# Taking one half-size dummy matmul out of the opening of an MLP kernel, between the transposes and layer 1

## The chip, the cores and the metric

The kernel runs on one core of one Trainium2 chip. The metric is device time in microseconds (us) for one execution; where several runs are compared, the mean or the median over runs is given and named. Early in execution the pace of the matmuls doubles (in the trace, pairs of 256 columns start 213 ns apart at first and 109 ns apart later) while the granted clock reads 1.0 throughout. "The clock doubles" means this change of pace below; whether it is a clock, no trace shows.

## The reference

```python
def reference(x, w1, b1, w2, b2):          # x: 1 x 2048 x 448, w1: 448 x 1792, w2: 1792 x 448, all bf16
    h = jnp.einsum("bsd,df->bsf", x, w1) + b1
    h = jax.nn.gelu(h, approximate=True)
    return jnp.einsum("bsf,fd->bsd", h, w2) + b2
```

## The kernel before

The 2048 tokens are worked in four chunks of 512. For the first chunk, x comes in its natural layout and is transposed on TensorE (twelve 128x128 transposes, and two more for the 64 remainder columns of D = 3 x 128 + 64). ScalarE and VectorE copy ("evacuate") the results from PSUM, where the kernel has TensorE put them, to SBUF, from where its layer matmuls read them. All layer matmuls then run as pairs on the two 64-row halves of the array (in the trace the two of a layer-1 pair start 2 to 6 ns apart).

While x is on its way, TensorE runs dummy matmuls of ones (from 0.78 us in the trace; x landed at 3.86). One more half-size dummy (256 columns) stands after the transposes.

```python
    HC = SC // 2          # 256; SC = 512
    NWARM = 7
    # ...
        def turn_b1():    # bias into its layout, on VectorE
            for q in range(4):
                pr.op("vector", lambda e, q=q: e.transpose(
                    b1t[32 * q:32 * q + 32, :], b1n[:, 32 * q:32 * q + 32]), after=["b1n"], event=("b1t", q))
            pr.op("vector", lambda e: e.tensor_copy(b1_f[:, :], b1t[:, 0:NFT]),
                  after=[("b1t", q) for q in range(4)], event="b1")

        def warm(n, cols=SC):
            for _ in range(n):
                pr.op("tensor", lambda e: e.matmul(unit[0][:, 0, 0:cols], lhsT=ones_w, rhs=ones_m[:, 0:cols],
                                                   start=True, stop=True))
    # ... in turn_all(): four x tiles, their evacuation on VectorE, ScalarE, VectorE, ScalarE in turn
            for t in range(STC):
                turn(t)
                evac(("vector", "scalar")[t % 2], t)
    # ... the two remainder transposes (L359), and their copies (L368)

        warm(NWARM)
        warm(1, HC)
        turn_all()
        warm(1, HC)       # the dummy in question
        turn_b1()

        for i in (0, 1):  # remainder weights, copied to the other 64 rows, on VectorE (L382)
            # ...
            pr.op("vector", lambda e, odd=odd: e.tensor_copy(odd(slice(0, H)), odd(slice(H, P))),
                  after=[("w1r", i)], event=("w1rU", i))
        L = [Layer1(0, j) for j in range(NPAIR)]
        for h in (0, HC):         # first the columns of x tiles 0 and 1, then those of 2 and 3
            L[0].a(h, h + HC)
            L[1].a(h, h + HC)
        L[0].b()                  # its first steps are on w1; the last of them needs the copied remainder weights
        # ...
```

Of the kernel before, what the change touches and what calls it, by code (L numbers as in the profile page):

```python
# [73 lines left out]
def bass_standalone__dense_activation_gelu__prompt_kernel(  # L74
# [13 lines left out]
    HC = SC // 2  # L88
# [9 lines left out]
    with ExitStack() as es:  # L98
# [79 lines left out]
        def turn_b1():  # L178
# [5 lines that stand above are left out]
# [5 lines left out]
# [4 lines that stand above are left out]
# [156 lines left out]
        def turn_all():  # L349


            pr.op("vector", lambda e: e.tensor_copy(  # L352
                xr[:, :, :].rearrange("p q (two h) -> p q two h", two=2),
                xn[:, :, D3:D].rearrange("p (q two) h -> p q two h", two=2)), after=["x"], event="xr_in")
# [3 lines that stand above are left out]
            for q in range(STC // 2):  # L358
                pr.op("tensor", lambda e, q=q: e.transpose(  # L359
                    stage(0)[:, q * P:(q + 1) * P], xr[:, q, :], ident[:, :]),  # L360
                    after=["xr_in", ("xT0", 0)], event=("xr", q))
            halves = (slice(0, H), slice(H, P))
            for src, engine in enumerate(("vector", "scalar")):
                i = stage(0)[halves[src], 0:2 * P].rearrange("p (q s) -> p q s", q=2)
                for dst in (src, 1 - src):
                    o = xT[halves[dst], KT, 0:SC].rearrange("p (q two s) -> p q two s", q=2, two=2)[:, :, src, :]
                    pr.op(engine, lambda e, o=o, i=i, engine=engine:
                          e.copy(o, i) if engine == "scalar" else e.tensor_copy(o, i),  # L368
                          after=[("xr", 0), ("xr", 1)], event=("xR0", dst, src))
            busy[(3, 0)] = ("xR0", 1, 0)  # L370
            busy[(3, 2)] = ("xR0", 0, 1)
# [1 line left out]
        warm(NWARM)  # L373
        warm(1, HC)
        turn_all()
        warm(1, HC)
        turn_b1()

        for i in (0, 1):
# [78 lines left out]
```

## Time and profile before

| | value |
|---|---|
| time, median of the 3 first runs | 94.28 us (94.17 to 94.35) |
| profiled execution | 94.75 us, span 93.4 us |
| TensorE (PE) busy | 90.4 us, 97% of the span |
| last transpose starts | 5.337 us |
| dummy starts | 5.444 us |
| first layer-1 matmul starts | 5.794 us |
| first matmul on the remainder weights starts (its twin, on the copied rows, 2 ns later) | 8.155 us |

The starts with three digits are single records of the trace; the views below show the same to 0.01 us.

The page of the kernel before begins with the busy time of each engine (us, share of the span, number of instructions):

```profile
span 93.4 us, 2060 instructions
## 1 busy us (share of the span) xinstructions
PE 90.4 (97%) x932; PEld 46.5 (50%) x932; DVE 13.3 (14%) x33; ACT 38.5 (41%) x63; POOL 1.7 (2%) x8
```

The chain of work that ended last, in order of time, for the kernel before (start, length, what):

```profile
7 pieces in order of time: start us, us, what
0.74 0.04 issue
0.78 3.36 PE u L191 x8
4.14 1.29 PE u L338 x12
5.43 0.21 PE u L359 x2
5.65 0.21 PE u L191
5.86 85.41 PE u L216 x909
91.27 0.38 DVE out_sb L325
```

Dummies (L191), transposes (L338, L359), the dummy in question (L191 again, 0.21 us), then layer matmuls (L216): but for the short first and last pieces it is all TensorE. So the dummy stands on this chain.

The timeline of the kernel before around the dummy (start, length, engine, line, operation; in brackets the idle time before it and what ended that):

```profile
5.23 0.42 PE L359 MATMUL u<-ident,xr 128*128 128x128 bf16 x2
5.34 0.15 PEld L191 LDWEIGHTS u<-const-bfloat16-1.0 128*128 128x128 bf16 x1
5.44 0.42 PE L191 MATMUL u<-const-bfloat16-1.0 128*128 128x256 bf16 x1
...
5.79 0.13 PEld L216 LDWEIGHTS u<-xT,w_sb 64*128 64x128 bf16 x4 [0.30 <-issue]
5.79 0.40 PE L216 MATMUL u<-xT,w_sb 64*128 64x256 bf16 x2
```

A matmul's length in this view overlaps the next one's (0.42 us for a dummy that takes 0.21 us of the chain), so distances between starts are what count. The weight load of layer 1 is late, after 0.30 us of idle on the loader, and the profile names nothing that it waited for.

### The profile page before, as it was taken

The numbers are of one execution on the slowest core, as the hardware profiler recorded it, in microseconds if no ns is written. First come the engines' busy times: TensorE is split into PE (matmuls) and PEld (weight loads), VectorE is DVE, ScalarE is ACT, GpSimd is POOL, SyncE is SP. The second block draws the span as 40 slices with busy tenths as digits, with TensorE's granted clock in tenths as the row PEclk, the third lists the DMA queues.
The fourth block names the chain that finished last, engine by engine and source line by source line (L and its number), as shares of the span: only waits on it lengthen the run. The fifth ranks groups of instructions, "written<-read, shape, count | busy, mean of one in ns | idle before, by whom it ended". The sixth has DMA issues, their size and how long they took to land.

```text
span 93.4 us, 2060 instructions
## 1 busy us (share of the span) xinstructions
PE 90.4 (97%) x932; PEld 46.5 (50%) x932; DVE 13.3 (14%) x33; ACT 38.5 (41%) x63; POOL 1.7 (2%) x8
## 2 busy tenths in 40 slices
PE   6999999999999999999999999999999999999990
PEld 2475444455544444454554444445544444475890
DVE  0173001010334000000234000000234000000421
ACT  6073787900002887900002888900001878910001
POOL 6000000000000000000000000000000000000000
DMA  2999999554748000000033000000022000000022
GB/s 51 358 275 292 360 309 151 113 113 91 83 86 217 7 0 0 7 0 0 0 102 101 0 0 4 0 7 0 0 98 98 0 0 7 0 0 7 18 80 98
DMA packets 12344, 7.32 MB, mean 78 GB/s; under 512 B 6960, under 2 KB 12144, under 8 KB 12336
## 3 DMA queue, kind: packets, MB, share of 16 engines
q1 hardware_dynamic: 11904, 6.80, 31.1%
q10 hardware_dynamic: 400, 0.39, 1.2%
q8 instruction: 7, 0.11, 0.5%
q14 instruction: 1, 0.01, 0.0%
q0 software_dynamic: 32, 0.00, 0.0%
HBM read 3.79 MB, written 1.84 MB: 60 GB/s over the span
## 4 chain that ended last, share of the span: by engine, by line
PE 97%; DVE 0%; issue 0%
PE u L216 91%; PE u L191 4%; PE u L338 1%; DVE out_sb L325 0%; PE u L359 0%
## 5 line engine op out<-in xcount | busy, mean ns | idle before, releaser
L268 ACT ACTIVATE g<-u,b_f 128x512 bf16<-128x512 f32 x56 | 35.0, 685 | 40.3 <-PE u L216 40.3
L216 PE MATMUL u<-w_sb,g 64*128 64x448 bf16 (+1 forms) x504 | 43.2, 328 | 0.0
L216 PE MATMUL u<-xT,w_sb 64*128 64x512 bf16 (+1 forms) x348 | 41.2, 372 | 0.0
L216 PEld LDWEIGHTS u<-w_sb,g 64*128 64x128 bf16 x504 | 24.4, 94 | 18.6
L216 PEld LDWEIGHTS u<-xT,w_sb 64*128 64x128 bf16 x348 | 16.9, 95 | 19.6 <-issue 0.3
L311 DVE TENSOR_TENSOR out_sb<-u,b_bc 128x448 bf16<-128x448 f32 x14 | 8.1, 619 | 60.6 <-PE u L216 60.6
L216 PE MATMUL u<-xT,w1r 64*128 64x512 bf16 x56 | 10.6, 376 | 0.0
L191 PE MATMUL u<-const-bfloat16-1.0 128*128 128x512 bf16 (+1 forms) x9 | 3.8, 578 | 0.8 <-PEq L443 0.8
L216 PEld LDWEIGHTS u<-xT,w1r 64*128 64x128 bf16 x56 | 2.7, 94 | 3.3
L328 ACT CAST out_sb<-u 128x224 bf16<-128x224 f32 x1 | 0.3, 346 | 9.2 <-PE u L216 9.2
L191 PEld LDWEIGHTS u<-const-bfloat16-1.0 128*128 128x128 bf16 x9 | 1.2, 138 | 2.4 <-issue 2.4
L345 ACT COPY xT<-u 128x384 bf16<-128x384 bf16 x2 | 1.0, 479 | 2.8 <-PE u L338 2.8
L175 ACT ACT_TABLE_LOAD x1 | 1.3, 1283 | 0.7 <-PEq L443 0.7
L338 PEld LDWEIGHTS u<-ident,xn 128*128 128x128 bf16 x12 | 1.2, 140 | 0.5 <-issue 0.5
L338 PE MATMUL u<-ident,xn 128*128 128x128 bf16 x12 | 1.4, 307 | 0.0
L186 DVE COPY xT<-xT 64x512 bf16<-64x512 bf16 x3 | 0.9, 290 | 3.5 <-DMA xT<-in_x_dram 3.5
L406 DVE COPY b_z<-b_bc 1x448 bf16<-1x448 bf16 x1 | 0.3, 267 | 6.8 <-DMA b_bc<-in_b_dram 6.8
L319 DVE TENSOR_TENSOR out_sb<-u,b_bc 128x448 bf16<-128x448 f32 x1 | 0.6, 625 | 1.7 <-PE u L216 1.7
L180 DVE STREAM_TRANSPOSE b1t<-b1n 32x32 bf16<-32x32 bf16 x4 | 0.8, 202 | 0.1
L345 DVE COPY xT<-u 128x384 bf16<-128x384 bf16 x2 | 0.7, 357 | 0.7 <-PE u L338 0.7
L368 ACT COPY xT<-u 64x256 bf16<-64x256 bf16 x2 | 0.7, 368 | 0.0
L352 DVE COPY xr<-xn 128x256 bf16<-128x256 bf16 x1 | 0.2, 227 | 3.0 <-DMA xn<-in_x_dram 3.0
(18 smaller groups left out, 5.0 us busy)
## 6 DMA issues: line engine op xcount, KB each, us to landing
out_dram<-out_sb SPq DMA_DIRECT2D x16, 112.0 KB, 1.7
w_sb<-in_w_dram SPq DMA_DIRECT2D x2, 784.0 KB, 8.7
w_sb<-in_w_dram SPq DMA_DIRECT2D x1, 576.0 KB, 6.4
xn<-in_x_dram SPq DMA_DIRECT2D x1, 448.0 KB, 3.1
w_sb<-in_w_dram ACTq DMA_DIRECT2D x1, 384.0 KB, 4.2
w_sb<-in_w_dram SPq DMA_DIRECT2D x1, 384.0 KB, 4.1
xT<-in_x_dram SPq DMA_TRANSPOSE x12, 4.5
w1r<-in_w_dram SPq DMA_DIRECT2D x1, 160.0 KB, 4.0
```

What stands on the lines that cost most here:

```text
L175: pr.op("scalar", lambda e: e.activation(junk[:, :], one, ACT.Gelu_apprx_tanh), event="table")
L180: pr.op("vector", lambda e, q=q: e.transpose(b1t[32 * q:32 * q + 32, :], b1n[:, 32 * q:32 * q + 32]), after=["b1n"], event=("b1t", q))
L186: pr.op("vector", lambda e: e.tensor_copy(xT[0:H, KT, s0:s1], xT[H:P, KT, s0:s1]), after=after, event=event)
L191: pr.op("tensor", lambda e: e.matmul(unit[0][:, 0, 0:cols], lhsT=ones_w, rhs=ones_m[:, 0:cols], start=True, stop=True))
L216: o = pr.op("tensor", lambda e: e.matmul(unit[u][:, lo, cols], lhsT=lhsT, rhs=rhs, start=start, stop=stop, skip_group_check=skip), after=a ...
L268: pr.op("scalar", lambda e, lo=lo, ft=ft: e.activation(g[:, ft, c * SC:(c + 1) * SC], unit[u][:, lo, :], ACT.Gelu_apprx_tanh, bias=b1_f[:, ...
L311: pr.op("vector", lambda e, lo=lo, j=j: e.tensor_tensor(out=out_sb[:, j, :], in0=unit[u][:, lo, 0:D], in1=b2_bc[:, :], op=ALU.add), after= ...
L319: pr.op("vector", lambda e: e.tensor_tensor(out=out_sb[:, j, :].rearrange("p (two h) -> p two h", two=2), in0=unit[u][:, :, 0:DH], in1=b2_ ...
L328: pr.op("scalar", lambda e: e.copy(out_sb[:, j, DH:D], unit[u][:, 1, 0:DH]), after=[y[1]], event=("o", j, 1))
L338: pr.op("tensor", lambda e, k=k: e.transpose(stage(t)[:, k * P:(k + 1) * P], xn[:, t, k * P:(k + 1) * P], ident[:, :]), after=["ident", "x ...
L345: pr.op(engine, lambda e: e.copy(o, i) if engine == "scalar" else e.tensor_copy(o, i), after=[("xt", t)], event=("xT0", t))
L368: e.copy(o, i) if engine == "scalar" else e.tensor_copy(o, i),
```

## The change

One line goes. The intent is to have layer 1 start earlier by what the dummy took.

```diff
         warm(NWARM)
         warm(1, HC)
         turn_all()
-        warm(1, HC)
         turn_b1()
```

The order of the instructions on the other engines stays as it was. Line numbers below it fall by one (L382 becomes L381).

## The prediction

> **What bounds the kernel now.** TensorE. Its busy line reads 90.4 of 93.4 us (97%); the chain that ended last is 97% TensorE. In the groups, the layer matmuls show 0.0 us of idle before them, their weight loads 0.3 us before the first. A nanosecond taken from the opening of TensorE reaches the end, unless something else holds the work.
>
> **What is removed.** One dummy matmul (ones, 128x256) and its weight load, between the last transpose and the first layer-1 matmul. Nothing is added; the other engines keep their instructions in the same order.
>
> **Its place, from the timeline between 5.2 and 8.6 us.** The last transpose starts at 5.34 us, the dummy at 5.44, the first layer-1 matmul at 5.79, 350 ns later. 256-column pairs at the same slow pace start 208 to 213 ns apart, so the dummy streams some 213 ns, and about 137 ns more pass. What the first layer-1 matmul needs is there earlier: the first w1 part landed at 4.99 us, ScalarE's evacuation ended at 5.31, the wait for it at 5.40. [...]this weight load starts only at 5.79, when elsewhere one starts with the matmul before. The drain would then follow the last transpose, and layer 1 start near 5.58 us, 0.21 earlier.
>
> **The clock.** The granted clock reads 1.00 throughout, but the pairs are 208 ns apart up to 6.62 us and 107 ns from 6.74 on. [...] If the doubling stays near 6.7 us, the 0.21 us gained is slow time: it holds one 256-column pair, worth 107 ns at the full rate. That is my central case: 0.11 us. If the doubling moves forward with the work, 0.21 us is offered.
>
> **The next limit.** VectorE copies the remainder weights of layer 1 to the other 64 rows after the bias; the copy ends at 7.85 us; the weight load that needs it starts at 7.94, its matmul at 8.155. VectorE does not move. 0.11 us earlier just fits (8.05); 0.21 us would lose about 0.1 to this wait. Both cases come to about 0.1 us.
>
> **Prediction.** 94.28 - 0.11 = 94.17, rounded up for a little waiting: **94.18 us**, range 93.95 to 94.50. Faster by over 2%: 0.01; within 2%: 0.97; slower by over 2%: 0.02. The range is the spread of the runs (0.18 us) plus a tail for the clock.
>
> **What would show each step.** First layer-1 matmul near 5.58 us, about 240 ns after the last transpose started: drain right; at 5.79: something else released it. The 107 ns spacing starting near 6.7 us: clock right. The first matmul with remainder weights near 8.05 us, later ones shifted alike, no new idle time on TensorE: the gain carried through.
>
> **What would make it wrong.** [...] Each microsecond that the doubling comes later costs half a microsecond[...]. I give a late clock about one chance in eight. If the first layer-1 matmul waits for something other than the drain, nothing is gained[...]. Run-to-run spread may hide 0.1 us in a median of three.

Marked as cut are passages on the hardware that no trace or run shows: the ground given for the 137 ns, a rule for the doubling of the pace, and what followed from that rule for a late clock. The sum: 94.28 - 0.11 = 94.17 us, put at 94.18; the one chance in eight for a late clock is the author's guess. "Drain" is only a name for the time, beyond the streaming, between the last 128-row operation and the first 64-row one (137 ns here). The "full rate" is the fast pace.

## The result, and the profile after

| | before | after |
|---|---|---|
| median, 6 runs each of the same rounds | 94.21 us (93.96 to 94.35) | 94.39 us (94.21 to 94.69) |
| ratio after / before | | 1.0026, 95% interval 1.0004 to 1.0049 |
| span of the profiled execution | 93.4 us | 93.2 us |

A ratio is the mean time of one kernel's fast runs over that of the other's of the same rounds, so it is not quite the ratio of the medians. By this first comparison the change is within 2%, and slower by 0.26%. The two profiled executions say the opposite: the one after is shorter by 0.2 us.

The page of the kernel after, and then its chain:

```profile
span 93.2 us, 2058 instructions
## 1 busy us (share of the span) xinstructions
PE 90.2 (97%) x931; PEld 50.5 (54%) x931; DVE 13.3 (14%) x33; ACT 38.5 (41%) x63; POOL 1.7 (2%) x8
```

```profile
8 pieces in order of time: start us, us, what
...
4.16 1.44 PE u L338 x12
5.60 0.20 PE u L359 x2
5.80 85.25 PE u L216 x899
```

The timeline of the kernel after around the place where the dummy was, and around the remainder weights:

```profile
5.40 0.41 PE L359 MATMUL u<-ident,xr 128*128 128x128 bf16 x2
...
5.73 0.22 PEld L216 LDWEIGHTS u<-xT,w_sb 64*128 64x128 bf16 x6 [0.18 <-issue]
5.73 0.39 PE L216 MATMUL u<-xT,w_sb 64*128 64x256 bf16 x4
...
7.70 0.74 PE L216 MATMUL u<-xT,w1r 64*128 64x512 bf16 x2
7.78 0.49 DVE L381 COPY w1r<-w1r 64x256 bf16<-64x256 bf16 x2
8.06 0.09 PEld L216 LDWEIGHTS u<-xT,w1r 64*128 64x128 bf16 x1 [0.47 <-DVE w1r L381]
```

Four things are to be seen.

1. The last transpose (5.503 us) and the first layer-1 matmul (5.733) are 230 ns apart, where they were 457 ns apart. So the dummy's time was given up.
2. The transposes came 0.17 us later than before (4.16 against 4.00), because x landed later (4.03 against 3.86 us). That is no effect of the change.
3. From the very first pair, layer 1 runs at the fast pace: its 256-column pairs start 120 and then 109 ns apart. Before, the first four distances were 186 to 214 ns.
4. There is a wait that the page of before does not have: the weight load of the copied remainder weights waited for VectorE (0.47 us of idle on the loader).

Points 3 and 4 raise the question. Did taking the dummy away change the clock, or do these two executions differ in the clock for another reason?

### The profile page after: what moved, and what is told of

The parts are those of the page before. It is cut to its first block, busy times and chain, and to the rows that moved or that the text cites. A ratio compares the mean times of both kernels' runs of the same rounds, so it can differ in the third digit from the quotient of the medians.

```text
span 93.2 us, 2058 instructions
## 1 busy us (share of the span) xinstructions
PE 90.2 (97%) x931; PEld 50.5 (54%) x931; DVE 13.3 (14%) x33; ACT 38.5 (41%) x63; POOL 1.7 (2%) x8
## 4 chain that ended last, share of the span: by engine, by line
PE 97%; ACT 0%; issue 0%
PE u L216 91%; PE u L191 4%; PE u L338 2%; ACT out_sb L328 0%; PE u L359 0%
## 5 line engine op out<-in xcount | busy, mean ns | idle before, releaser
L216 PE MATMUL u<-w_sb,g 64*128 64x448 bf16 (+1 forms) x504 | 43.9, 328 | 0.0
L216 PE MATMUL u<-xT,w_sb 64*128 64x512 bf16 (+1 forms) x348 | 42.9, 369 | 0.0
L216 PEld LDWEIGHTS u<-w_sb,g 64*128 64x128 bf16 x504 | 28.1, 94 | 14.7
L216 PEld LDWEIGHTS u<-xT,w_sb 64*128 64x128 bf16 x348 | 19.7, 94 | 18.7 <-issue 0.2
L216 PE MATMUL u<-xT,w1r 64*128 64x512 bf16 x56 | 16.5, 376 | 0.0
L216 PEld LDWEIGHTS u<-xT,w1r 64*128 64x128 bf16 x56 | 5.3, 94 | 3.7 <-DVE w1r L381 0.5
```

What stands on the lines that cost most here:

```text
L216: o = pr.op("tensor", lambda e: e.matmul(unit[u][:, lo, cols], lhsT=lhsT, rhs=rhs, start=start, stop=stop, skip_group_check=skip), after=a ...
```

## The experiments

Three theories stood at the start.

- **Clock theory.** Without the dummy the doubling of the pace comes later in some runs. That would explain the 0.26%.
- **Stall theory.** Layer 1 starts earlier, but then meets VectorE's copy of the remainder weights, and the gain is lost there.
- **Spread.** The doubling comes at any time whatever the kernel does. The 0.26% is chance.

### The same two kernels again

again_before is the kernel before, again_after the kernel after, both unchanged.

> The unchanged kernel against itself: ratio 1.000, which shows how far a ratio of five rounds strays with no cause (I expect within 0.2%). Its trace is a second draw of the time at which the 256-column pairs go from 208 to 107 ns apart: if that time is tied to the program it is again 6.6 to 6.7 us; if it runs freely it is another one, and the span moves by half of the difference.

> The changed kernel once more. If the 0.26% of the first comparison is real, the ratio is 1.002 to 1.004 again; if it was [...]the runs' spread, it is 0.998 to 1.001. In its trace the drain is still about 230 ns from the last transpose to the first layer-1 matmul, and the matmul on the copied remainder weights again waits for VectorE's copy.

| | runs, us | median | ratio to the kernel before, 95% interval |
|---|---|---|---|
| again_before | 93.92 93.94 93.94 93.96 94.30 94.54 | 93.95 | 0.9976 (0.9948 to 1.0005) |
| again_after | 93.91 94.10 94.16 94.48 94.58 94.74 | 94.32 | 0.9995 (0.9962 to 1.0029) |

The kernel before against itself came out at 0.9976. That is nearly as far from 1 as the first result of the change, on the other side. Its 11 control runs reached from 93.99 to 94.81 us. So a ratio of this size proves nothing here, although the interval of the first comparison left out 1.

The traces show why. These are the transposes of four executions (count, then shortest, median and longest duration in ns, then first and last start): the kernel before, its second trace, the kernel after, its second trace.

```profile
L338 PE MATMUL u<-ident,xn x12: 264/311/311, 4.0 to 5.1; 128*128 128x128 bf16 x12
```

```profile
L338 PE MATMUL u<-ident,xn x12: 216/219/220, 3.9 to 4.5; 128*128 128x128 bf16 x12
```

```profile
L338 PE MATMUL u<-ident,xn x12: 263/311/311, 4.2 to 5.3; 128*128 128x128 bf16 x12
```

```profile
L338 PE MATMUL u<-ident,xn x12: 267/314/315, 4.0 to 5.1; 128*128 128x128 bf16 x12
```

In the second trace of the kernel before, the transposes start 55 to 56 ns apart instead of 106 to 107: the pace had doubled before they began. By the first spacing at the fast pace, the doubling came at about 6.6 us in the first trace of the kernel before and about 3.7 us in its second. In the two traces of the kernel after it came at about 5.6 and 6.5 us. With and without the dummy it comes early and late. Over all seven traces without a hold (three more follow below), it came before the first layer-1 matmul in five. What sets the moment, the traces do not show. The two traces of the kernel before (94.75 and 93.92 us) differ by 0.83 us: 0.11 us is x landing earlier (3.75 against 3.86 us), and the rest lies in the stretch where their pace differs, less what the later waits described below took back.

One pair of these traces has nearly the same clock: the first of the kernel before and the second of the kernel after. Here is the group of the 256-column layer-1 matmuls in each (instructions from 3 to 9 us; busy, mean ns), first before, then again_after:

```profile
L216 PE MATMUL u<-xT,w_sb 64*128 64x256 bf16 x24 | 1.9, 315 | 0.0
```

```profile
L216 PE MATMUL u<-xT,w_sb 64*128 64x256 bf16 x24 | 1.9, 322 | 0.0
```

From the last transpose to the last matmul of the kernel it is 85.625 us in the first and 85.465 us in the second, 160 ns less. The spacings put the doubling about 0.12 us earlier in the second (my interpolation), which is worth 60 ns. What is left, about 0.10 us, is what the prediction gave to its central case. In an execution whose clock doubles late, the dummy was worth that, as far as one pair of traces and an interpolation can tell.

### The copy of the remainder weights before the bias

Here VectorE makes the first of its two copies of remainder weights before it turns the bias.

```diff
         turn_all()
         warm(1, HC)                     # only in w1r_first_dummy
-        turn_b1()
 
         for i in (0, 1):
+            if i:
+                turn_b1()
```

> Dummy kept; VectorE copies the first part of the remainder weights before the bias, so the copy ends near 6.7 us and not 7.85. If the stall on that copy limits the kernel before too whenever the clock doubles early (stall theory), 0.1 to 0.4 us faster than the kernel before; if the copy never matters with the dummy there, ratio 1.000.

> The same early copy without the dummy. Stall theory: with the stall gone, removing the dummy now pays, so about 0.1 us faster than w1r_first_dummy and 0.2 to 0.5 us faster than the kernel before. Clock theory[...]: slower than w1r_first_dummy by some 0.25 us, as the changed kernel was than the kernel before.

| | runs, us | median | ratio to the kernel before, 95% interval |
|---|---|---|---|
| w1r_first_dummy | 93.95 94.10 94.15 94.24 94.35 94.64 | 94.20 | 0.9991 (0.9963 to 1.0019) |
| w1r_first_none | 93.73 94.01 94.02 94.09 94.17 94.35 | 94.05 | 0.9972 (0.9946 to 0.9999) |

The order of the two fits the stall theory and not the clock theory, but they overlap. Times alone cannot settle a tenth of a microsecond here. In both traces the remainder matmuls run without any wait; the one on the copied rows starts 1.97 us after layer 1's first. In the second trace of the kernel before it took 2.22 us: that execution, with the dummy, waited for the copy too. The stall was no product of the change. All four traces with the late copy in which the clock had doubled before layer 1 show it (again_before, after, and below hold_dummy and hold_none).

The second trace of the kernel before shows one more wait. These are two groups of its page; after the second bar stand the loader's idle time, what ended most of it, and how much that was:

```profile
L216 PEld LDWEIGHTS u<-xT,w_sb 64*128 64x128 bf16 x348 | 17.0, 94 | 19.0 <-DMA w_sb<-in_w_dram 0.5
L216 PEld LDWEIGHTS u<-xT,w1r 64*128 64x128 bf16 x56 | 3.0, 94 | 3.7 <-DVE w1r L382 0.4
```

The last part of w1 landed at 10.50 us, and the matmuls on it started at 10.55, after 0.34 us of idle on the loader. With this wait it is 85.057 us from the first layer-1 matmul to the last matmul; hold_dummy below, which meets the copy but not the load, has 84.938. So in an execution that is early enough, this load takes back what the opening gains. How often that happens is not shown.

### A hold that takes the clock out of the comparison

To see 0.1 us, the clock must have doubled before the part that is compared. These kernels run 26 dummies instead of 7, and the transposes wait for a long memset on GpSimd, which ended at 8.58 us in all four traces. In the first trace of the kernel before, the first part of w1 and the remainder weights landed by 7.49 us; layer 1 of these kernels starts at 9.88 us or later.

```diff
-    NWARM = 7
+    NWARM = 26
+    HOLD = 7200
+        idle = sb("idle", [P, HOLD], BF16)
+        pr.op("gpsimd", lambda e: e.memset(idle[:, :], 0.0), event="hold")
-                    after=["ident", "x"], event=("xt", t) if k == KT - 1 else None)
+                    after=["ident", "x", "hold"], event=("xt", t) if k == KT - 1 else None)
```

> Tool to take the clock out of the comparison: 26 dummies in place of 7 at the start, and the transposes wait for a long memset on GpSimd, so that layer 1 opens some 5 us later, with all loads landed and the clock long doubled. Some 99 us; all pairs of layer 1 107 ns (256 columns) or 213 ns (512) apart from the first on. Spread of identical runs well under the 0.9 us that the kernel before shows, if that spread was the clock. The dummy between transposes and layer 1 is kept; with it the matmul on the copied remainder weights should wait some 30 ns for VectorE, as in the second trace of the kernel before.

> The same without the dummy. Stall theory: layer 1 starts 0.107 us earlier, and the matmul on the copied remainder weights waits some 0.14 us instead of 0.03, so the time is that of hold_dummy within 0.06 us. Clock theory: the clock is doubled long before, so no difference either, but then without a longer stall, so 0.107 us faster. Plain saving: 0.107 us faster.

> With the dummy, and the copy of the remainder weights before the bias on VectorE. Stall theory: the copy is over more than 1 us before it is needed, so at most 0.05 us faster than hold_dummy.

> Without the dummy and with the early copy. Stall theory: no stall, so 0.107 us (the dummy's 256 columns at the full rate) faster than hold_first_dummy, and the fastest of the four. If removing the dummy costs time by something else than the stall, it is not faster than hold_first_dummy.

The runs fall in two groups. In most the memset is what the transposes wait for, and then they repeat within 0.06 us ("held" below). In the others the 26 dummies outlasted the memset, because the clock doubled late (by the spacing of the dummies, after 6.1 us in the four traces of this kind and at 4.6 to 4.8 us in the three held ones). The profiled executions show both kinds: the transposes start at 8.73 us in held executions, and at 9.25 us in the profiled one of hold_dummy, which took 99.16 us. A run more than 0.06 us above the fastest of its kernel is put with the rest; this limit was set after the runs, and only the profiled ones are known to be of one kind or the other from a trace.

| | held runs, us | their mean | the other runs |
|---|---|---|---|
| hold_dummy | 98.60 98.62 98.65 98.66 | 98.63 | 99.16 99.22 |
| hold_none | 98.61 98.61 98.61 98.62 | 98.61 | 98.76 99.15 |
| hold_first_dummy | 98.47 98.49 | 98.48 | 99.10 99.11 99.22 99.24 |
| hold_first_none | 98.45 98.46 98.46 98.46 98.48 | 98.46 | 99.12 |

So with a fast clock the dummy is worth about 0.02 us, with the late copy (where the held runs of one kernel alone differ by 0.06) and with the early one. The early copy is worth 0.15 us, with the dummy and without. In the trace of hold_dummy the second half of the first remainder pair started 249 ns after the first half (2 ns in the first trace of the kernel before), and from layer 1's first matmul to the kernel's last it took 162 ns longer than in hold_first_dummy (84.938 against 84.776 us, in the table below). The stall is real, but it does not explain where the dummy's 107 ns went: I had expected hold_first_none to gain all of it. That part of the stall theory fell.

The traces add up, also where the hold was overrun, since all four ran the compared part at the fast pace:

| | last transpose to first layer-1 matmul | that to the last matmul | sum, us |
|---|---|---|---|
| hold_dummy | 258 ns | 84.938 us | 85.196 |
| hold_none | 231 ns | 84.968 us | 85.199 |
| hold_first_dummy | 258 ns | 84.776 us | 85.034 |
| hold_first_none | 230 ns | 84.777 us | 85.007 |

Removing the dummy brings layer 1 forward by 27 or 28 ns and not by 107. With the late copy even this is given back at the stall (84.968 against 84.938). So something else holds layer 1's start when the dummy is gone. In the trace of hold_none the weight load of layer 1 starts at 9.854 us. A wait for ScalarE ended at 9.829, and ScalarE had finished its evacuation of the second x tile at 9.740. These are timeline lines of hold_dummy around the dummy and layer 1's start, and then of hold_none:

```profile
10.23 0.27 PE L194 MATMUL u<-const-bfloat16-1.0 128*128 128x256 bf16 x1
10.43 0.10 PEld L219 LDWEIGHTS u<-xT,w_sb 64*128 64x128 bf16 x2 [0.16 <-issue]
10.43 0.28 PE L219 MATMUL u<-xT,w_sb 64*128 64x256 bf16 x2
```

```profile
9.26 0.48 ACT L348 COPY xT<-u 128x384 bf16<-128x384 bf16 x1 [7.03 <-PE u L341]
...
9.65 0.22 PE L362 MATMUL u<-ident,xr 128*128 128x128 bf16 x1
9.85 0.13 PEld L219 LDWEIGHTS u<-xT,w_sb 64*128 64x128 bf16 x2 [0.16 <-issue]
9.88 0.27 PE L219 MATMUL u<-xT,w_sb 64*128 64x256 bf16 x1
```

The profile says "issue" for this wait, and it says the same, with the same 0.16 us, in hold_dummy, where the dummy fills the time. So the mark alone does not tell the two apart, and it needed a test.

There is a hint without a hold as well. From the end of that evacuation to the first layer-1 matmul it is 145 ns in hold_none (9.740 to 9.885) and also in w1r_first_none (5.295 to 5.440). There the clock doubled during the transposes, and layer 1 started 375 ns after the last of them. The profile names the load of w1 for this wait; that landed at 5.325, too close to tell from the trace alone.

### A shorter evacuation on ScalarE

Tile 1 has three blocks of 128 columns. ScalarE now copies two; the third goes to a bank of another PSUM unit, from where VectorE copies it.

```diff
+        def alt():
+            return unit[1][:, 1, 0:2 * P].bitcast(BF16)[:, 0:P]
...
-                    stage(t)[:, k * P:(k + 1) * P], xn[:, t, k * P:(k + 1) * P], ident[:, :]),
+                    alt() if (t, k) == (1, 2) else stage(t)[:, k * P:(k + 1) * P], xn[:, t, k * P:(k + 1) * P], ident[:, :]),
...
+            k1 = 2 if t == 1 else KT          # evac() copies k1 blocks
+            if t == 1:
+                pr.op("vector", lambda e: e.tensor_copy(xT[:, 2, P:2 * P], alt()),
+                      after=[("xt", 1)], event=("xT0", 1, 2))
+                busy[(1, 2)] = ("xT0", 1, 2)
```

Layer 1 waits for the new event as well. hold_first_5x is the control: hold_first_dummy with `warm(2)` added after the dummy.

> hold_first_dummy, with ScalarE's evacuation of the second x tile cut to two of its three blocks; VectorE copies the third from another bank. If this evacuation is what layer 1 waits for only when the dummy is gone, nothing changes here: the held runs stay at 98.48 us within 0.03, and the first layer-1 matmul starts 0.25 to 0.26 us after the last transpose.

> The same without the dummy. If the evacuation was what hid the dummy, layer 1 now starts about 0.15 us after the last transpose (128 columns at the full rate, 53 ns, and a drain of some 97 ns, read from the dummy at the full rate) in place of 0.23, and the held runs are near 98.38 us: 0.10 below hold_split_dummy and 0.08 below hold_first_none. If something else held it, 98.46 as before.

> Control: hold_first_dummy with two full dummies more at the same place, 1024 columns. If the opening of layer 1 stands on TensorE's path once the dummies outlast the evacuation, the held runs are 0.43 us slower than hold_first_dummy (two times 216 ns), at 98.91 us; if that place has slack for some other reason, less.

> The version that these reasons point to, without the hold: no dummy, early copy of the remainder weights, cut evacuation. 0.2 to 0.35 us faster than the kernel before in the mean of its runs (0.15 from the stall when the clock doubles early, 0.03 to 0.1 from the dummy, 0.08 from the evacuation), with runs spread over 0.6 us or more by the clock, so that the interval may still touch 1.

| | held runs, us | the other runs | last transpose to first layer-1 matmul | sum to the last matmul, us |
|---|---|---|---|---|
| hold_split_dummy | 98.48 98.49 98.49 98.49 98.49 98.49 | none | 258 ns | 85.034 |
| hold_split_none | 98.38 | 98.66 98.85 98.96 99.03 99.14 | 149 ns | 84.924 |
| hold_first_5x | 98.93 98.93 | 99.17 99.38 99.46 99.49 | 696 ns | 85.471 |

This is the timeline of hold_split_none. ScalarE's copy is 0.37 us instead of 0.48, and layer 1 starts 149 ns after the last transpose:

```profile
9.74 0.37 ACT L352 COPY xT<-u 128x256 bf16<-128x256 bf16 x1 [7.50 <-PE u L344]
...
10.07 0.27 PE L370 MATMUL u<-ident,xr 128*128 128x128 bf16 x2
...
10.28 0.10 PEld L219 LDWEIGHTS u<-xT,w_sb 64*128 64x128 bf16 x2
10.28 0.28 PE L219 MATMUL u<-xT,w_sb 64*128 64x256 bf16 x1
```

With the dummy, the shorter evacuation changes nothing (258 ns, 85.034 us, both as in hold_first_dummy). Without it, layer 1 starts 149 ns after the last transpose, and the whole is 110 ns shorter than with the dummy: the 107 ns that were missing. Only one run of hold_split_none was held, but it says the same: 98.38 against 98.49. The control cost 0.45 us (98.93 against 98.48), near the two dummies' 0.43. So once dummies outlast the evacuation, TensorE's path is what counts at this place.

split_none, the version without a hold that these reasons point to, ran 93.90 to 94.59 us, median 94.17, ratio 0.9987 (0.9956 to 1.0018). Its mean is 0.12 us below the kernel before, with an interval from 0.41 faster to 0.17 slower, so the expected 0.2 to 0.35 us is neither shown nor excluded; the runs again spread over 0.7 us. Its trace shows the wait for the last part of w1 again (landed at 10.60 us, 27 ns lost). No version was shown to beat both kernels. w1r_first_none came nearest, with an interval that ends at 0.9999.

## Why the prediction was right or wrong

The measured 94.39 us lies in the range of 93.95 to 94.50, and "within 2%" was right. That says little for the mechanism: the six runs of the unchanged kernel in the same rounds (93.96 to 94.35) lie in that range too. The central saving of 0.11 us was not what the runs gave. All runs together, taken over several chips and rounds, are 45 of the kernel before with a mean of 94.28 us and 12 of the kernel after with 94.37. The difference, +0.09 us, has a standard error of 0.08 us (from the spreads of 0.28 and 0.25 us). It is no effect that can be told from zero. The 95% interval, -0.07 to +0.26 us, does not hold the predicted -0.11 either, though it mixes chips and rounds.

- **Bound by TensorE: right.** Both chains are 97% TensorE.
- **The drain follows the last transpose: right.** Expected about 240 ns after the last transpose at the slow pace; measured 246 ns (again_after) and 230 ns in the first trace of after, whose clock doubled at that moment. Beyond the streaming time some 139 ns pass at the slow pace (246 less 107; after the dummy in the first trace of before, 350 less 213, it was 137). At the fast pace it is 96 ns (149 less 53, half of 107, in hold_split_none; 203 less 107 after the dummy in hold_dummy). So the gap was there after a transpose and after a dummy alike. No run changed only the number of rows, so its cause is not shown.
- **"If the doubling stays near 6.7 us": the step that failed.** It is the term that was mis-sized. The prediction took one execution's moment as typical, with a one-in-eight chance for a later clock; an earlier one it weighed only as moving forward by the 0.21 us gained. The traces of these two kernels have it between about 3.7 and 6.6 us, early as often as late. Where it comes late, the saving is about 0.10 us, as predicted (one pair of traces). Where it has come before the transposes, it is 27 to 28 ns at the start of layer 1, because ScalarE's evacuation then holds the start; that was shown by shortening it, in the kernels with a hold. No trace without a hold shows the changed kernel with a clock that early. The prediction had this wait as over at 5.40 us and in the past, which holds where the pace is slow, as in that trace (layer 1 at 5.79 us).
- **"Both cases come to about 0.1 us": wrong.** VectorE's copy was rightly named as the next limit. But with a fast clock it is a limit already with the dummy (2.22 us from layer 1's start to the remainder matmul instead of 1.97), and it gives back the 27 ns: 85.196 and 85.199 us.
- **"No new idle time on TensorE": not as told.** The page of after has 0.5 us of idle on its loader for that copy. It comes with the early clock of that execution; the second trace of the kernel before has 0.4 us of it, with the dummy.
- **"The range is the spread of the runs (0.18 us)": wrong.** Three runs showed 0.18 us; 45 runs of the same kernel spread over 0.98 us (93.85 to 94.83).
- **The clock theory** is not needed: without the dummy the doubling also came early (5.6 us). It is not excluded that the dummy shifts the average moment of the doubling: the runs leave room for a loss of up to 0.26 us. That stays open, and so does how much of the 0.98 us spread is the clock and how much is when x and w1 land, since the hold takes out both.

## What to carry to other kernels

Before believing a tenth of a microsecond, run the unchanged kernel against itself, and compare several traces: if the pace of the matmuls doubles at a different moment in each (here between about 3.7 and 6.6 us), hold the compared part back until after the doubling. A dummy that fills TensorE while another engine finishes something cost here only what it outlasted that wait by (27 or 28 ns of 107), so look for that wait, also when the profile calls it "issue". And when an early engine becomes faster, read the slack of every other producer again: it was measured at the slow pace (the copied remainder weights, with no wait in the first trace of the kernel before, had one in its second). That holds for the loads too: the last part of w1 became a limit only in the two unheld traces whose layer 1 started first (5.07 and 5.42 us).
